# Delta-rule attention with a routed feed-forward layer: block 1's squares kept on chip, later blocks' squares and the zeroing moved in the written order

## The chip, the cores and the metric

One core of one Trainium2 chip runs the whole kernel. The metric is the device time of one launch in microseconds (us). The kernel before took 520.19 us (median of 3 runs, 515.07 to 524.5). A smaller number is better.

## The reference

For each of 4 batches and 8 heads (32 pairs, called lanes) a state of 48 x 48 is carried over 768 tokens. Keys are divided by their norm; at each token the output is read from the state, and then the state is corrected:

```
k_n = k / (norm(k) + 1e-6)
y[t]  = q[t] @ state
state = state + beta[t] * outer(k_n[t], v[t] - state.T @ k_n[t])
```

The heads' outputs, side by side, give 3072 tokens of width 384. A router (384 x 8) picks one of 8 experts for each token by the largest logit; the token's output is `gate * (relu(x @ w1[e]) @ w2[e])`, with w1 of 384 x 1024 and w2 of 1024 x 384, and the gate the softmax weight of the chosen expert.

## The kernel before

**Tiling.** The 768 tokens are 6 blocks of 128; a block is four sub-chunks of 32. A unit n = 4 * block + batch is one block of one batch, 24 in all; their tiles have that number (kt8 holds the keys of unit 8, gg8 its Gram). The main loop has 27 ticks t; a unit n passes through four ticks, sub-chunk q in tick n + q, so that four units are in work at a time. A tick has seven places, and place 7t + i is where `beside(t, i)` (L1121) writes extra work between the tick's own instructions.

**One tick.** `residual` (L490) multiplies keys with the states and with earlier corrections into the PSUM tile ks; VectorE (DVE) subtracts ks from the values v_all (L515). `chunk(ks_, t)` writes the Gram of a later unit (`kpart`, L249): 16 matmuls at L296, two ScalarE (ACT) copies at L278. `apply` (L517) multiplies the residual with wt, the inverted 32 x 32 triangular system of each lane (L523), and ACT copies the result out (L527). `finish` reads out y and updates the state; `qpart` makes the masked q-k products; `emit_x` forms the routed row. In ticks 0 to 3 the values of the next tick are scaled by ACT (L476, eight small instructions), later by DVE (L479).

**The inverses.** wt of a block is made on DVE, mostly by `Inverse` (L1009): `prepare` (norms out of the squared lengths, L342 to L369), `columns` (L395, L398) and `lanes` (products L421, reductions L427, a last transpose L432). Its steps are written a few at a time at the places, by a budget of 0.86 to 0.92 us each; what is left is written in one piece before `residual` of the tick that first needs wt (ticks 4, 8, 12, 16, 20). When the next block's inverse is ready too, the two alternate. `ROOT` names for each block three places: where `squares` is written (L318; its DVE instruction, L320, waits for the tile lg), where `root` is written (an ACT square root, L324), and from where the inverse may step. Block 0's inverse is made ahead of tick 0, with its last quarter by matmuls (`corner_products`, L438; L457, L464 on TensorE, L459, L468 on ACT).

**The squares' way.** lg holds, one lane beside the other, the 32 x 32 diagonal pieces of the Grams. For blocks 1 to 5 the last `kpart` of the block sends these pieces from gg to DRAM by four DMAs of 128-byte runs (gd, L284) and reads them back in the other layout by one DMA (lg, L288), which waits until the four have landed. All direct DMAs are issued by SyncE in written order: an instruction that waits holds back the loads of keys, queries, values and ku behind it. `KAT` gives the tick of a Gram's making where it is not n - 10.

**Zeroing.** The DRAM rows that routed tokens are gathered in (xg) are zeroed by seven DMAs of 788 KB each (L201): one behind gd of block 1, one behind gd of block 2, one each at the ends of ticks 2 and 4, one of tick 6 and two of tick 7.

**Before tick 0.** `fill` (L973) writes the Grams 4 to 7 of block 1 and 0 and 1 of block 0, each but the last with 13 or 12 idle matmuls (L777) behind it, beside block 0's columns on DVE. GpSimd (POOL) makes constants, masks (L307) and zeroes tiles, and `norms` lets it copy four 32 x 32 pieces into nt_all (L369), which the scaling of values needs. Behind the ticks the experts run, nearly bound by TensorE (PE) alone.

Of the kernel before, what the change touches and what calls it, by code (L numbers as in the profile page):

```python
# [8 lines left out]
F32 = mybir.dt.float32  # L9
# [9 lines left out]
B, H, S, D = 4, 8, 768, 48  # L19
C = 128  # L20
NT = S // C
NB = C // 32
# [19 lines left out]
def deltanet_moe(ctx, tc, kt_d, qt_d, kn_d, v_d, beta_d, w_gate, w1, w2, out):  # L42
    nc = tc.nc
# [67 lines left out]
    GB = 3  # L111
    KSL = 16
    LEAD = 10
    KAT = {8: 0, 9: 0, 2: 1, 10: 1, 3: 2, 11: 2, 12: 3, 13: 3}
    QSL = 4
    KTL = 17
    QTL = 6
# [2 lines left out]
    NB_ = 2  # L120
    LIVE = 7
    LAG = NB - 1
    FILL = 'k4 k5 k6 k7 k0', 'k1', '', ''

    ROOT = {1: (0, 1, 2), 2: (24, 27, 29), 3: (42, 45, 47), 4: (70, 73, 75), 5: (98, 101, 103)}
    FD = {"k4": 13, "k5": 13, "k6": 13, "k7": 13, "k0": 12}
    INIT = (0, 1, 2, 3, 'l', 'l', 'l')

# [3 lines left out]
    SPEND0 = (0.92,) * 7  # L132
    SPEND = (0.9,) * 7
    SPEND2 = (0.86,) * 7
    CL = (0, (0, 1), (0, 1))
    CLT = (2, 4)
    CLU = (6, 7, 7)
    W1 = 4
    DM2 = 0
    DEF = 2  # L140
# [18 lines left out]
    fp = ep_.enter_context(tc.tile_pool(name="fp", bufs=1, side="right"))  # L159
# [12 lines left out]
    gg_t = [gg_g[j // B][:, j % B] for j in range(KSL)]  # L172
# [13 lines left out]
    tiles = {tb: {b: {} for b in range(B)} for tb in range(NT)}  # L186
# [9 lines left out]
    def clear_slots(k):  # L196
        for x in [slots.pop(0) for _ in range(k)]:
            zero(x)
# [19 lines left out]
    def load_q(n):  # L218
        if n < NT * B:
            load_rows(qt_t[n % QTL], qt_d[n], n < QTL)  # L220
# [10 lines left out]
    def rows(t):  # L231

        if t < NB:
            return [slice(0, 32 * (t + 1))]
        return {NT * B: [slice(32, 64), slice(64, 128)], NT * B + 1: [slice(64, 128)],
                NT * B + 2: [slice(96, 128)]}.get(t, [slice(0, 128)])
# [13 lines left out]
    def kpart(n):  # L250

        tb, b = n // B, n % B
        kt, gg = kt_t[n % KTL], gg_t[n % KSL]
        V, A = nc.vector.tensor_copy, nc.scalar.copy
        if tb == 0:
            if n == 0:
                tiles["dg"] = fp.tile([128, BH, 32], F32, name="dg", tag="lg", bufs=3)
            dg = tiles["dg"]
            w = 64 if b < WIDE else 32
            db = [psg_[-1].tile([128, NP, w], F32, name=f"db{b}_0", tag="g"),  # L260
                  pss.tile([128, NP, w], F32, name=f"db{b}_1", tag="y", bufs=YB) if b < 2 else
                  pss.tile([128, NP, w], F32, name=f"db{b}_1", tag=f"sum{b - 2}")]
            for h in range(H):
                p, a = h // 2, h % 2
                r = slice(64 * a, 64 * a + 64)
                for i in range(0, C, w):
                    t = slice(i, i + w)
                    nc.tensor.matmul(db[a][t, p, :], lhsT=kt[r, p, t], rhs=kt[r, p, t], start=True, stop=True,
                                     tile_position=(64 * a, i), skip_group_check=True)
            for i in range(0, w, 32):  # L270
                for t in range(i, C, w) if w > 32 else (slice(0, C),):
                    t = t if w == 32 else slice(t, t + 32)
                    V(out=dg[t, b * H:(b + 1) * H:2], in_=db[0][t, :, i:i + 32])
                    A(out=dg[t, b * H + 1:(b + 1) * H:2], in_=db[1][t, :, i:i + 32])
            yield
        pg = halves(f"pg{tb}_{b}", kt, kt)
        for a in range(2):
            A(out=gg[:, a:H:2], in_=pg[a])  # L278
        if tb > 0 and b == B - 1:
            early_ = CL[tb] if tb < len(CL) else (0, 0)  # L280
            clear_slots(early_[0])
            for i in range(NB):
                r = slice(32 * i, 32 * i + 32)
                nc.sync.dma_start(out=gd[tb].rearrange("(i n) (r c) -> i r n c", i=NB, r=32)[i],  # L284
                                  in_=gg_g[tb % (KSL // B)].rearrange("p b h c -> p (b h) c")[r, :, r])
            tiles[tb]["lg"] = fp.tile([128, 32, 32], F32, name=f"lg{tb}", tag="lg", bufs=3)
            clear_slots(early_[1])
            nc.sync.dma_start(out=tiles[tb]["lg"].rearrange("p r c -> p (r c)"), in_=gd[tb])  # L288

    def halves(nm, kt, xt):  # L290

        pg = [psg_[-1].tile([128, NP, C], F32, name=f"{nm}_{a}", tag="g") for a in range(2)]
        for p in range(NP):
            for a in range(2):
                r = slice(64 * a, 64 * a + 64)
                nc.tensor.matmul(pg[a][:, p], lhsT=kt[r, p], rhs=xt[r, p], start=True, stop=True,  # L296
                                 tile_position=(64 * a, 0), skip_group_check=True)
        return pg

    def qpart(n):  # L300

        tb, b = n // B, n % B
        pm = pm_t[n % QSL]
        pg = halves(f"pq{tb}_{b}", kt_t[n % KTL], qt_t[n % QTL])
        for a in range(2):
            nc.scalar.copy(out=pm[:, a:H:2], in_=pg[a])  # L306
        nc.gpsimd.affine_select(out=pm, in_=pm, compare_op=ALU.is_gt, fill=0.0, base=0,  # L307
                                pattern=[[0, H], [1, C]], channel_multiplier=-1)
        yield

    def clear_w(tb):
        lw = tiles[tb]["lw"] = fp.tile([128, 32, 32], F32, name=f"lw{tb}", tag="lw", bufs=2)
        nc.gpsimd.memset(lw, 0.0)

    def squares(tb):

        T = tiles[tb]
        for k in ("ss", "s0", "r0"):  # L318
            T[k] = lp.tile([128, 32], F32, name=f"{k}{tb}", tag=k)
        nc.vector.tensor_scalar(out=T["ss"], in0=T["lg"].rearrange("p a b -> p (a b)")[:, 0:1024:33],  # L320
                                scalar1=1e-36, scalar2=None, op0=ALU.max)

    def root(tb):
        nc.scalar.activation(out=tiles[tb]["s0"], in_=tiles[tb]["ss"], func=AF.Sqrt, scale=0.25)  # L324
# [146 lines left out]
    def scale_v(t, act=False):  # L471

        vn = vt[t]
        for r in rows(t):
            for h in range(H if act else 0):
                nc.scalar.activation(out=vn[r, h], in_=vn[r, h], func=AF.Copy, scale=nt_t[r, t * H + h:t * H + h + 1])  # L476
            if act:
                continue
            nc.vector.tensor_tensor(out=vn[r], in0=vn[r], in1=nt_t[r, t * H:(t + 1) * H].unsqueeze(2)  # L479
                                    .broadcast_to([r.stop - r.start, H, D]), op=ALU.mult)  # L480
# [277 lines left out]
    def run(gen, steps=1):  # L758

        for _ in range(steps):  # L760
            if next(gen, tiles) is tiles:
                return False
        return True
# [8 lines left out]
    def dummy(k, w=512):  # L772

        if k:
            wm = pss.tile([128, w], F32, name=f"wm{next(cnt)}", tag="y", bufs=YB)
        for _ in range(k):
            nc.tensor.matmul(wm, lhsT=busy[:, 0:128], rhs=busy[:, 0:w], start=True, stop=True)  # L777
# [163 lines left out]
    clear_w(0)  # L941

    ks_ = [(KAT.get(n, n - LEAD), kpart(n), n) for n in range(NN)]
    qs_ = [(n - QSL + NB, qpart(n)) for n in range(NN)]
    dummy(5)
# [20 lines left out]
    for n in range(NB_):  # L966
        load_ku(n)
    clear_slots(CL[0])
    while "nt" not in tiles[0]:
# [6 lines left out]
    def fill(xs):  # L976
        for x in xs.split():
            n, part = int(x[1:]), (ks0 if x[0] == "k" else qs0)
            if part[n] and not run(part[n]):
                done.add(x)  # L980
            dummy(FD.get(x, 0), 16)

    fill(FILL[0])
    for n in range(LEAD, LEAD + 2):
        load_k(n)
    router()
    fill(FILL[1])
    lane = columns(0)
    run(lane, 12)
    for _ in norms(0):  # L990
        pass
    scale_v(0, act=True)
    run(lane, 100)
    turns = corner_products(0)
    run(turns)
    fill(FILL[2])
    run(turns)
    fill(FILL[3])
    ks_ = sorted((x for i, x in enumerate(ks_) if f"k{i}" not in done), key=lambda x: (x[0], x[2]))
    qs_ = [x for i, x in enumerate(qs_) if f"q{i}" not in done]  # L1000
    class Inverse:
# [13 lines left out]
        def ready(self, t):  # L1015
            if self.at == -12:
                return place[0] >= ROOT[self.tb][2]
            return not ("cols" in tiles[self.tb] and t < B * self.tb - 1)
# [43 lines left out]
    def beside(t, i):  # L1062

        place[0] = 7 * t + i
        for tb in ROOT:
            if place[0] == ROOT[tb][0]:
                squares(tb)
            if place[0] == ROOT[tb][1]:
                root(tb)
# [10 lines left out]
    for t in range(NN + LAG):  # L1080
# [43 lines left out]
        if t >= LAG:  # L1124
            load_q(t - LAG + QTL)
        clear_slots(CLT.count(t))
        clear_upper(CLU.count(t))
    i = 0
# [181 lines left out]
    if True:  # L1310
        ind, sel, t8 = small("ind"), small("sel"), small("t8")
        ei, j0, ce, r, rc, gi, ov = (small(n_, (128, 1)) for n_ in ("ei", "j0", "ce", "r", "rc", "gi", "ov"))
# [63 lines left out]
        for f in range(KF):  # L1376
# [4 lines left out]
                                     in_=yo, in_offset=None, bounds_check=N - 1, oob_is_err=False)  # L1381
# [40 lines left out]
```

## Time and profile before

| | before |
|---|---|
| median of 3 runs | 520.19 us |
| the profiled execution | 521.66 us |
| its span, first to last instruction | 519.9 us |
| mean granted TensorE clock | 0.946 |
| PE busy | 469.9 us, 90% |
| DVE busy | 311.9 us, 60% |
| ACT busy | 270.8 us, 52% |
| POOL busy | 157.0 us, 30% |

The profiled execution lies 1.47 us above the median; 1.76 us of it are outside the span. In the timelines and tables below times are in us from the span's start. A granted clock of 1.00 is 2.4 GHz, and of 0.5 is 1.2 GHz; a value between means that a stretch had both. PE is busy nearly everywhere, so what one looks for are the stretches in which it is not, or in which its clock is low.

### The profile page before, as it was taken

How to read it: one execution, taken by the hardware profiler on the slowest of the kernel's cores; microseconds unless marked ns; L12 is line 12 of the kernel's file. 1: busy time of each engine (PE TensorE's matmuls, PEld its weight loads, DVE VectorE, ACT ScalarE, POOL GpSimd, SP SyncE). 2: the span in 40 equal slices, each digit the busy share in tenths (PEclk: the TensorE clock that was granted, in tenths of full speed). 3: DMA queues.
4: the chain of work that ended last, by engine and by line, in shares of the span. 5: the costliest groups of instructions: out<-in, count | busy, mean ns of one | idle time of the engine just before them, and what ended most of it. 6: DMA issues, size and time to landing. Idle time of an engine off the chain costs nothing. (4 is left out here: it accounts for less than half of the span.)

```text
span 519.9 us, 18283 instructions
## 1 busy us (share of the span) xinstructions
PE 469.9 (90%) x7724; PEld 432.9 (83%) x7724; DVE 311.9 (60%) x717; ACT 270.8 (52%) x600; POOL 157.0 (30%) x342
## 2 busy tenths in 40 slices
PE   6898869788789669997889999999999999999995
PEld 4788758677677558786679899999999999999995
DVE  5839495798487498954554386646382746436330
ACT  4567845565547436576644255645363636344330
POOL 6111124477446556873030211020201111110202
PEclk9869979999879978998999989999999999999999
DMA  8780765974724713363431156655364746354001
GB/s 244 183 239 4 198 178 127 272 201 108 198 76 102 168 65 109 95 222 122 119 100 57 38 171 203 183 172 177 115 212 127 224 129 198 126 178 127 35 3 43
DMA packets 57151, 73.39 MB, mean 141 GB/s; under 512 B 25929, under 2 KB 44831, under 8 KB 57056
## 3 DMA queue, kind: packets, MB, share of 16 engines
q1 hardware_dynamic: 53600, 62.44, 42.4%
q0 software_dynamic: 3456, 9.57, 5.1%
q8 instruction: 75, 1.23, 1.0%
q14 instruction: 20, 0.16, 0.1%
HBM read 54.15 MB, written 18.62 MB: 140 GB/s over the span
## 5 line engine op out<-in xcount | busy, mean ns | idle before, releaser
L861 PE MATMUL y<-w2h,hx 128*128 128x384 f32 x352 | 93.5, 340 | 0.1
L864 POOL DMA_INDIRECT out_dram<-yo,idx x32 | 30.7, 959 | 198.8 <-ACT yo L1201 96.0
L784 DVE TENSOR_TENSOR w2l<-w2r,w2h 128x768 fp32r<-128x768 f32 x32 | 31.3, 980 | 72.9 <-ACT w2h L783 72.7
L861 PEld LDWEIGHTS y<-w2h,hx 128*128 128x128 f32 x352 | 64.1, 188 | 0.4 <-issue 0.4
L527 ACT COPY u<-ks 32x384 f32<-32x384 f32 x96 | 45.1, 470 | 34.3 <-PE ks L523 32.7
L861 PE MATMUL y<-w2l,hx 128*128 128x384 f32 x176 | 59.3, 337 | 0.0
L850 PE MATMUL h<-xl,w1h 128*128 128x416 f32 (+2 forms) x168 | 57.3, 341 | 0.2 <-DVE xl L784 0.2
L850 PE MATMUL h<-xh,w1h 128*128 128x416 f32 (+2 forms) x168 | 57.3, 341 | 0.0
L850 PE MATMUL h<-xh,w1l 128*128 128x416 f32 (+2 forms) x168 | 57.2, 341 | 0.0
L853 ACT ACTIVATE hx<-h 128x448 fp32r<-128x448 f32 (+1 forms) x64 | 32.8, 517 | 33.3 <-PE h L850 32.4
L1201 ACT ACTIVATE yo<-y,gt 128x384 f32<-128x384 f32 x22 | 12.8, 582 | 69.1 <-PE y L861 57.8
L523 PE MATMUL ks<-v_all,wt 32*32 32x48 f32 x1536 | 28.7, 222 | 22.0 <-DVE v_all L515 21.5
L307 POOL TENSOR_SCALAR_AFFINE_SELECT pm<-pm 128x1024 f32<-128x1024 f32 x24 | 27.1, 1131 | 67.7 <-ACT pm L306 67.5
L496 PE MATMUL ks<-st,kt 128*32 128x96 f32 x768 | 43.7, 250 | 3.2 <-issue 1.7
L523 PEld LDWEIGHTS ks<-v_all,wt 32*32 32x32 f32 x1536 | 24.5, 119 | 25.9 <-DVE v_all L515 23.4
L854 DVE SCALAR_TENSOR_TENSOR hx<-h,hx 128x448 fp32r<-128x448 f32 (+1 forms) x64 | 36.8, 586 | 14.6 <-ACT hx L853 14.4
L296 PE MATMUL pg<-kt 64*128 64x128 f32 x384 | 35.6, 318 | 2.6 <-ACT gg L278 1.6
L496 PEld LDWEIGHTS ks<-st,kt 128*32 128x32 f32 x768 | 32.4, 110 | 6.5 <-ACT u L527 1.9
L278 ACT COPY gg<-pg 128x512 f32<-128x512 f32 x48 | 25.8, 588 | 20.9 <-PE pg L296 20.1
L599 POOL DMA_INDIRECT xg<-row,sli x24 | 28.4, 1182 | 25.9 <-ACT yt L570 8.0
L784 DVE TENSOR_TENSOR w1l<-w1r,w1h 128x1024 fp32r<-128x1024 f32 x24 | 29.4, 1224 | 9.8 <-ACT w1h L783 6.5
L296 PEld LDWEIGHTS pg<-kt 64*128 64x128 f32 x384 | 30.2, 218 | 5.5 <-ACT gg L278 2.5
(205 smaller groups left out, 1050.3 us busy)
## 6 DMA issues: line engine op xcount, KB each, us to landing
w1r<-in_w_dram SPq DMA_DIRECT2D x24, 512.0 KB, 3.6
w2r<-in_w_dram SPq DMA_DIRECT2D x32, 384.0 KB, 3.5
xg<-zrow SPq DMA_DIRECT2D x7, 788.0 KB, 6.8
kt<-in_kt_dram SPq DMA_DIRECT2D x17, 256.0 KB, 5.8
xr<-xg SPq DMA_DIRECT2D x7, 591.0 KB, 5.0
ku<-in_kn_dram SPq DMA_DIRECT2D x20, 192.0 KB
qt<-in_qt_dram SPq DMA_DIRECT2D x36, 96.0 KB, 2.6
v_all<-in_v_dram SPq DMA_DIRECT2D x15, 192.0 KB
```

The costliest lines, as they stand in the source:

```text
L296: nc.tensor.matmul(pg[a][:, p], lhsT=kt[r, p], rhs=xt[r, p], start=True, stop=True, tile_position=(64 * a, 0), skip_group_check=True)
L307: nc.gpsimd.affine_select(out=pm, in_=pm, compare_op=ALU.is_gt, fill=0.0, base=0, pattern=[[0, H], [1, C]], channel_multiplier=-1)
L496: nc.tensor.matmul(ks[32 * q:32 * q + 32, 2 * p:2 * p + 2, :], lhsT=kt_t[n % KTL][:, p, 32 * q:32 * q + 32], rhs=st_view(n % B, p), start= ...
L523: nc.tensor.matmul(ks[r, h, :], lhsT=tiles[n // B]["wt"][r, n % B * H + h, :], rhs=vn[r, h, :], start=True, stop=True, tile_position=(32 * ...
L527: nc.scalar.copy(out=uview(n)[r], in_=ks[r])
L599: put = nc.gpsimd.indirect_dma_start(out=xg, out_offset=bass.IndirectOffsetOnAxis(ap=at, axis=0), in_=x, in_offset=None, bounds_check=OFF ...
L784: nc.vector.tensor_tensor(out=lo, in0=src, in1=hi.bitcast(F32), op=ALU.subtract)
L850: nc.tensor.matmul(ps, lhsT=w[:, d, fs], rhs=x_[:, d], start=(n == 0), stop=(n == len(terms) - 1))
L853: nc.scalar.activation(out=hh, in_=ps, func=AF.Relu)
L854: nc.vector.scalar_tensor_tensor(out=hl, in0=ps, scalar=0.0, in1=hh.bitcast(F32), op0=ALU.max, op1=ALU.subtract)
L861: nc.tensor.matmul(ps, lhsT=h(f)[h_], rhs=w2[w][:, f, :], start=(n == 0), stop=(n == len(terms) - 1))
L864: nc.gpsimd.indirect_dma_start(out=out, out_offset=bass.IndirectOffsetOnAxis(ap=idx, axis=0), in_=yo, in_offset=None, bounds_check=N - 1, ...
```

## The change

Block 1's squares no longer go through DRAM. Behind each Gram of block 1 GpSimd copies the four 32 x 32 diagonal pieces of its eight heads together (16 copies of 32 x 256 in all) into the tile of Gram 12, which is not yet in use, and DVE transposes it into lg (`compact`), behind the first part of `corner_products`. Its squares and root are written there too, and its inverse may step from place 0.

The Gram 7 is written behind block 0's norms, and Grams 0 and 1 behind the scaling of tick 0's values; the idle matmuls become 48 columns wide instead of 16. Grams 10 and 11 are made in tick 1, 2 and 12 in tick 2, 3 and 13 in tick 3. The squares, root and first step of blocks 3, 4 and 5 are written some five places later. The seven zeroings go to the ends of ticks 0 (two), 1, 2 (two) and 3 (two).

```diff
-    KAT = {8: 0, 9: 0, 2: 1, 10: 1, 3: 2, 11: 2, 12: 3, 13: 3}
+    KAT = {8: 0, 9: 0, 10: 1, 11: 1, 2: 2, 12: 2, 3: 3, 13: 3}
...
-    FILL = 'k4 k5 k6 k7 k0', 'k1', '', ''
-
-    ROOT = {1: (0, 1, 2), 2: (24, 27, 29), 3: (42, 45, 47), 4: (70, 73, 75), 5: (98, 101, 103)}
+    FILL = 'k4 k5 k6', 'k7', 'k0 k1'
+
+    ROOT = {1: (-1, -1, -1), 2: (24, 27, 29), 3: (47, 49, 51), 4: (75, 77, 79), 5: (103, 105, 107)}
...
-    CL = (0, (0, 1), (0, 1))
-    CLT = (2, 4)
-    CLU = (6, 7, 7)
+    CL = (0, (0, 0), (0, 0))
+    CLT = (0, 0, 1, 2)
+    CLU = (2, 3, 3)
...
-        if tb > 0 and b == B - 1:
+        if tb == 1:
+            sq = gg_t[KSL - B]
+            for i in range(NB):
+                r = slice(32 * i, 32 * i + 32)
+                nc.gpsimd.tensor_copy(sq.rearrange("p h (g c) -> p (h g) c", c=32)[r, b * H:(b + 1) * H], gg[r, :, r])
+        if tb > 1 and b == B - 1:
...
+    def compact(tb):
+
+        lg = tiles[tb]["lg"] = fp.tile([128, 32, 32], F32, name=f"lg{tb}", tag="lg", bufs=3)
+        nc.vector.transpose(out=lg, in_=gg_t[KSL - B].rearrange("p h (g c) -> p c (h g)", c=32))
...
-            dummy(FD.get(x, 0), 16)
+            dummy(FD.get(x, 0), 48)
...
-    fill(FILL[1])
     lane = columns(0)
     run(lane, 12)
     for _ in norms(0):
         pass
+    fill(FILL[1])
     scale_v(0, act=True)
+    fill(FILL[2])
     run(lane, 100)
     turns = corner_products(0)
     run(turns)
-    fill(FILL[2])
+    compact(1)
+    squares(1)
     run(turns)
-    fill(FILL[3])
+    root(1)
```

## Rows read from the trace of the kernel before

**Rows 1.** Page, part 1: busy time, share of the span, instructions of an engine.

```profile
PE 469.9 (90%) x7724; PEld 432.9 (83%) x7724; DVE 311.9 (60%) x717; ACT 270.8 (52%) x600; POOL 157.0 (30%) x342
```

**Rows 2.** Table of stretches (start:end): length, busy times, granted clock, DMA.

```profile
core 0: us, PE busy (x) PEld busy (x) DVE busy (x) ACT busy (x) POOL busy (x), PEclk, DMA share, GB/s
25.90:62.65 36.75, 33.42 (x968) 29.63 (x961) 22.94 (x53) 27.65 (x81) 5.65 (x12) 0.86 0.51 142
62.65:78.70 16.05, 10.84 (x234) 9.36 (x233) 12.41 (x29) 7.79 (x22) 3.33 (x7) 0.79 0.73 192
78.70:86.90 8.20, 7.86 (x236) 6.88 (x234) 5.75 (x22) 5.72 (x14) 3.55 (x11) 1.00 0.55 144
...
95.10:107.60 12.50, 9.64 (x234) 8.32 (x232) 12.47 (x23) 6.29 (x16) 6.20 (x9) 0.86 0.77 224
...
126.70:134.90 8.20, 7.96 (x238) 6.97 (x237) 1.67 (x2) 5.29 (x13) 5.88 (x20) 1.00 0.65 128
134.90:150.70 15.80, 11.65 (x234) 10.02 (x232) 13.54 (x22) 6.75 (x17) 4.97 (x13) 0.68 0.54 153
...
167.95:174.86 6.91, 6.91 (x225) 6.09 (x224) 1.29 (x2) 4.18 (x11) 4.51 (x14) 1.00 0.60 135
174.86:189.45 14.59, 8.23 (x218) 7.12 (x216) 12.25 (x23) 5.59 (x15) 5.28 (x11) 0.77 0.53 129
189.45:199.80 10.35, 8.23 (x223) 7.16 (x221) 9.80 (x27) 4.79 (x12) 6.95 (x21) 0.84 0.21 63
...
62.65:107.60 44.95, 36.30 (x934) 31.54 (x932) 32.56 (x78) 25.53 (x65) 17.99 (x41) 0.89 0.69 185
```

**Rows 3.** Waits: PE's from 20 to 250, then DVE's; us, times, longest.

```profile
PE ks L523 <- DVE v_all L515: 20.2, 7, 4.5
...
DVE ss L320 <- DMA lg<-gd: 28.3, 5, 7.5
```

**Rows 4.** Timeline of DVE: the squares of blocks 1 to 5; start, duration, instruction.

```profile
30.95 0.19 DVE L320 TENSOR_SCALAR ss<-lg 128x32 f32<-128x32 f32 x1 [3.57 <-DMA lg<-gd]
...
64.78 0.19 DVE L320 TENSOR_SCALAR ss<-lg 128x32 f32<-128x32 f32 x1 [5.19 <-DMA lg<-gd]
...
94.39 0.19 DVE L320 TENSOR_SCALAR ss<-lg 128x32 f32<-128x32 f32 x1 [5.14 <-DMA lg<-gd]
...
136.62 0.19 DVE L320 TENSOR_SCALAR ss<-lg 128x32 f32<-128x32 f32 x1 [7.55 <-DMA lg<-gd]
...
177.17 0.19 DVE L320 TENSOR_SCALAR ss<-lg 128x32 f32<-128x32 f32 x1 [6.88 <-DMA lg<-gd]
```

**Rows 5.** Timeline of PE: the first product with block 1's inverse, in tick 4.

```profile
71.93 1.51 PE L523 MATMUL ks<-v_all,wt 32*32 32x48 f32 x64 [4.49 <-DVE v_all L515]
```

**Rows 6.** Timeline of SyncE's queue: block 2's squares out and back.

```profile
51.10 3.27 SPq L284 DMA_DIRECT2D gd<-gg  x4
...
59.06 0.34 SPq L288 DMA_DIRECT2D lg<-gd  x1
```

**Rows 7.** Timeline ahead of tick 0: ACT on Gram 7, its scaling, a DVE transpose.

```profile
18.91 1.07 ACT L278 COPY gg<-pg 128x512 f32<-128x512 f32 x2 [0.57 <-PE pg L296]
...
23.18 1.91 ACT L476 ACTIVATE v_all<-v_all,nt_all 32x48 f32<-32x48 f32 x8
...
8.51 1.94 DVE L334 STREAM_TRANSPOSE lg<-dg 128x1024 f32<-128x1024 f32 x1
```

**Rows 8.** Timeline: GpSimd's work and DVE's two-input instructions beside it.

```profile
17.20 1.19 POOL L369 COPY nt_all<-r 32x32 f32<-32x32 f32 x4 [6.78 <-DVE r L365]
...
17.37 0.29 DVE L395 TENSOR_TENSOR tmp<-lg,lw 128x128 f32<-128x128 f32 x1
...
38.27 1.09 POOL L307 TENSOR_SCALAR_AFFINE_SELECT pm<-pm 128x1024 f32<-128x1024 f32 x1
...
38.44 1.04 DVE L395 TENSOR_TENSOR tmp<-lg,lw 128x96 f32<-128x96 f32 x1
39.51 0.26 DVE L398 TENSOR_TENSOR lw<-lw,tmp 128x96 f32<-128x96 f32 x1
```

## The prediction

> **What bounds the kernel now.** The page's busy shares come first [rows 1]: PE is at 90%, DVE at 60%, so as a mean the kernel is PE's. The table by ticks shows where that fails [rows 2]. An undisturbed tick takes 8.20 us at clock 1.00, or 6.91 when no Gram is left to make; tick 4 takes 16.05, tick 7 12.50, tick 11 15.80, tick 15 14.59 and tick 16 10.35, at clocks of 0.68 to 0.86. So what is lost there is lost twice: PE waits, and the clock is then part of the time at the lower level of 1.2 GHz. The wait lists name the link [rows 3]: PE waited 20.2 us for DVE's subtraction, and DVE 28.3 us, five times, for lg, the squares coming back from DRAM. The timeline has these five [rows 4]. DVE works in written order, so while L320 waits for lg, the rest of the running inverse and the next subtraction stand behind it. Four ticks of DVE work are 32.56 us (the last stretch of [rows 2]), against 4 x 8.20 = 32.8 of undisturbed PE: DVE has nothing to spare, and what it waits, PE pays at the block's end. Tick 4 shows it: block 2's squares hold DVE until 64.78, block 1's inverse comes late, and PE starts the product with it at 71.93 after 4.49 idle [rows 4, 5].
>
> **Before tick 0.** GpSimd gets 16 copies of 32 x 256, 12 of them ahead of the norms' copies. The trace has none of that size. Bounds: 0.30 us each (four of 32 x 32 in 1.19) and 1.09 (a select of 1024 columns) [rows 8]; I take 0.5, nearer the small one, as 256 columns are a quarter of 1024. Gram 6 was copied out by ACT at 18.34 (0.57 ahead of Gram 7's copies [rows 7]); its four pieces end at 20.3 and the norms' copies at 21.5, where they ended at 18.4. The scaling now stands in ACT's queue behind Gram 7 (19.98) and ahead of Grams 0 and 1. It runs 21.5 to 23.4, the two Grams' copies to about 26 (2 x 1.07, and PE's Gram 1 waits for a buffer of Gram 0), where ACT had been through with all of it at 25.1. So tick 0 starts 1.1 us late; with copies of 0.30 it is 0.3, with 1.09 it is 3.4. Gram 7's pieces end at 23.5, ahead of DVE's transpose (1.94 [rows 7]), which fills time in which DVE stood idle; the squares were late till 30.95 [rows 4], and that wait of 3.57 goes. The wider idle matmuls lie in PE's gaps; I cost them at nothing, bounds -1 to +1, for what the clock does. In SyncE's queue the four gd DMAs of block 1, a zeroing and the lg read that waited for them go; the loads behind them come sooner, and the two zeroings of tick 0 stand behind every load that ticks 0 and 1 need.
>
> **Ticks 0 to 3** have DVE busy 22.94 of 36.75 us, ACT 27.65 [rows 2]: a chain through ACT, whose work is the same. They keep their length. Block 1's inverse starts some 4 us earlier at least and has two places more.
>
> **Tick 4.** Grams 10 and 11 in tick 1 send block 2's squares out one tick earlier, about 8.5 us. Before, from the first DMA to landing took 64.78 - 51.10 = 13.7 us, with a zeroing between gd and lg [rows 6, 4]; none stands there now. So lg is there at 56 to 57, and DVE comes to the squares at 59.6 (64.78 - 5.19). The 5.19 us wait goes, and the remaining inverse fits in front of tick 4's subtraction. Tick 4 takes 8.45 instead of 16.05: 7.6 us won. Grams 2 and 3 only change places with them (16 matmuls, two ACT copies each), so a tick's load stays. SyncE now waits in tick 1 for Gram 11 and then for gd to land, and the loads of keys 13 and 14 and three zeroings stand behind: I expect key 13 at about 57, when tick 3 needs it (bounds: 0, or 1 us late; I take 0).
>
> **The later steps.** Blocks 3, 4 and 5 kept DVE waiting from 2.4 us into ticks 6, 10 and 14, until 7.5, 9.9 and 9.2 us into them [rows 4, 2]. Five places of 0.9 (0.86 in block 5) bring 4.5 us (4.3) of real inverse work in front, so DVE arrives at 6.9 (6.7): waits of 0.6, 3.0 and 2.5 are left of 5.14, 7.55 and 6.88. What is behind the wait is now close: two places, then the next subtraction. In tick 6 landing plus two places (1.8) is 9.3, before the subtraction's turn at 10: free. Tick 7 falls from 12.50 to 8.3: 4.2 won. In tick 10 it is 11.7, with the subtraction 12.3; PE needs it at 12.1. Tick 11 loses 0.2; as block 4's inverse starts four places later, more of block 3's stands in one piece at tick 12, 9.7 us of DVE work against 8.2, which costs 1.4. Ticks 10 and 11, 24.0 before, become 18.0: 6.0 won. In ticks 14 to 16 the undisturbed tick is 6.91, DVE's 10.4 of work in tick 15 does not fit, and I get 3 x 6.91 + 1.8 (squares) + 3.1 (work) + 1.4 (lower clock) = 27.0 instead of 31.85: 4.85 won. Block 5's later start costs about 0.5 at tick 20.
>
> **Sum:** 7.6 + 4.2 + 6.0 + 4.85 - 1.1 - 0.5 = 21.05 us, from 521.66: 500.6, said as 501. The experts behind are PE's own and move as a whole. That execution lies 1.5 us above the median shown; the three runs span 9.4, so I leave it there and add 4 us at the range's ends.
>
> **A rule against the change.** Beside GpSimd's select at 38.27 a DVE instruction with two SBUF inputs took 1.04 us, its neighbour of the same size 0.26; but beside the four small copies at 17.20 such a one took 0.29, no longer than elsewhere [rows 8]. I count no contention. The Trainium skill (GPSIMD Engine Reference, section 1, Specifications) says that GpSimd shares its SBUF interfaces with VectorE and that instructions with two SBUF inputs contend; block 0's columns, beside which the copies run, are of this kind. The first of the two rows agrees with it, the second does not. This is the third rival below.
>
> **Rivals.**
> First, DVE stays full: the squares still land late and, now right in front of a subtraction, hold it. For: lg needed 9.9 and 9.2 us in ticks 10 and 14, and there is no slack in the 32.56. Against: in tick 6 it landed at 7.5. Then blocks 4 and 5 win nothing: 521.66 - 7.6 - 4.2 + 1.1 = 511. Chance 0.16.
> Second, with the zeroing gone from ticks 4 to 7 and block 1's small packets gone, lg lands in ticks 10 and 14 as in tick 6, at 7.5: the left waits go, each followed by its share of lower clock: some 4 us more, 497. Chance 0.12.
> Third, the copies hold block 0's columns: 12 x 0.5 = 6 us on DVE, of which about 2 hide behind ACT's longer way, so tick 0 is 4 us later still: 505. Chance 0.12.
> Fourth, it doesn't do what it says for block 2: three zeroings, at the ends of ticks 1 and 2, run beside lg and the loads of keys 13 and 14, and tick 3 or 4 waits for them as long as before: 521.66 - 13.5 = 508. Against: SyncE issues the lg read ahead of them. Chance 0.06.
> Fifth, slower: GpSimd's strided copies are far dearer. They stand ahead of the norms, on which ACT's scaling and behind it Grams 0 and 1, the corners and tick 0 wait. POOL had 6.78 us idle there [rows 8], so 12 copies of c us push tick 0 back by 12c - 6.8. All that is won, 22 us, is gone at c = 2.4; at c = 3 it is 29.2, or 529. Against: the longest row beside it is 1.09 for four times the columns. Chance 0.04.
>
> **Numbers.** The forecast, 501, has 0.50, with 495 to 507 of its own. The range 493 to 512 runs from the second rival less 4 us to just past the first; it leaves out the fifth and the runs' far ends. About what a measurement can tell from no change is 2%, 10.4 us, so faster means under 509.8: nearly all of the forecast, second and third, somewhat under half of the first and over half of the fourth: 0.82. Slower than 530.6 is the fifth with yet dearer copies or a bad start: 0.04. Within 2%: 0.14.
>
> **What would show it.** In the changed trace: GpSimd copies of about 0.5 us at the new line and DVE's columns beside them no longer than 0.29; tick 0 at 26 to 28; L320 of block 1 at about 27 with no wait, that of block 2 with none, those of blocks 4 and 5 with 2 to 3 us; ticks 4 and 7 near 8.3 at clock 1.00, tick 15 still long. The prediction is wrong if PE still idles over 2 us for L515 in tick 4, if tick 0 starts after 30, or if ticks 11 and 15 keep their 15.80 and 14.59.

## The result and the profile after

The changed kernel takes 514.61 us (median; 508.67 to 517.6) where the kernel before took 519.85 (515.07 to 525.79) on the same chip: a ratio of 0.988, 95% interval 0.985 to 0.991. Medians and ranges are over all executions, but ratios compare only those in the faster of two states that executions fall into, so here and below a ratio is not the quotient of the two medians. It is faster by 1.2%, less than the 2% that I had called measurable, and outside the predicted range. The profiled execution took 512.92 us (span 510.7), against the 521.66 that the sum was made from: 8.7 us won instead of 21.05. (It lies 1.7 below its median, the one of before 1.8 above; that is the difference between 8.7 and 5.2.)

The page's busy line of the changed kernel, as [rows 1]:

```profile
PE 469.9 (92%) x7724; PEld 432.5 (85%) x7724; DVE 315.8 (62%) x718; ACT 270.7 (53%) x600; POOL 171.6 (34%) x358
```

POOL has 16 instructions and 14.6 us more; the compacting copies are 6.5 of it, the rest is spread over GpSimd's other instructions and was not followed up. PE is busy for the same time to the tenth, so the 9.2 us that the span lost are PE's idle time. The table of stretches shows where (columns as in [rows 2]); a stretch is a tick, and the first row is ticks 0 to 3 together, then ticks 4, 7, 8, 11, 15, 16 and 19:

```profile
27.40:66.10 38.70, 35.15 (x973) 31.02 (x961) 27.97 (x61) 27.61 (x81) 7.11 (x12) 0.82 0.38 98
...
66.10:79.90 13.80, 9.96 (x236) 8.47 (x234) 6.88 (x22) 7.92 (x23) 3.25 (x7) 0.88 1.05 302
...
96.50:105.90 9.40, 8.36 (x234) 7.27 (x232) 7.75 (x14) 5.90 (x16) 6.97 (x12) 1.00 0.86 211
105.90:117.20 11.30, 9.60 (x238) 8.39 (x236) 10.82 (x29) 6.02 (x15) 6.99 (x22) 0.85 0.33 99
134.50:144.10 9.60, 8.32 (x237) 7.09 (x237) 8.33 (x15) 6.04 (x16) 5.84 (x13) 1.00 0.77 200
167.90:175.70 7.80, 7.07 (x218) 6.03 (x216) 7.54 (x14) 4.84 (x14) 6.91 (x10) 1.00 0.96 245
175.70:189.20 13.50, 9.84 (x225) 8.43 (x226) 11.81 (x30) 5.06 (x13) 7.57 (x24) 0.75 0.25 71
203.80:214.00 10.20, 8.72 (x221) 7.39 (x219) 9.91 (x13) 4.87 (x13) 7.12 (x17) 0.83 0.35 112
```

Against [rows 2] tick 11 fell from 15.80 to 9.60, tick 15 from 14.59 to 7.80 and tick 7 from 12.50 to 9.40: the later steps work. Tick 4 only fell from 16.05 to 13.80. Ticks 0 to 3 grew from 36.75 to 38.70, and ticks 8, 16 and 19 are longer than they were (9.3, 10.35 and 8.2). The wait lists of the changed kernel, PE's first, as [rows 3] (20 to 250 us; total, times, longest):

```profile
PE ks L533 <- DVE v_all L525: 8.9, 5, 3.1
PE ks L506 <- issue: 2.9, 3, 2.3
PE yp L556 <- issue: 2.6, 2, 1.6
...
DVE ss L330 <- DMA lg<-gd: 1.5, 3, 0.8
```

DVE's wait for the squares is down from 28.3 to 1.5, PE's for DVE from 20.2 to 8.9. What has grown is "issue", PE standing still for nothing that the profile can name. The kernel before had these two at the same products:

```profile
PE ks L496 <- issue: 1.7, 2, 1.3
...
PE yp L546 <- issue: 0.3, 1, 0.3
```

The five squares on DVE's timeline, as [rows 4]:

```profile
29.22 0.19 DVE L330 TENSOR_SCALAR ss<-lg 128x32 f32<-128x32 f32 x1
...
62.47 0.17 DVE L330 TENSOR_SCALAR ss<-lg 128x32 f32<-128x32 f32 x1
...
96.43 0.19 DVE L330 TENSOR_SCALAR ss<-lg 128x32 f32<-128x32 f32 x1 [0.39 <-DMA lg<-gd]
...
134.02 0.19 DVE L330 TENSOR_SCALAR ss<-lg 128x32 f32<-128x32 f32 x1 [0.81 <-DMA lg<-gd]
...
168.34 0.19 DVE L330 TENSOR_SCALAR ss<-lg 128x32 f32<-128x32 f32 x1 [0.26 <-DMA lg<-gd]
```

Block 2's squares, at 62.47, wait for nothing: the wait of 5.19 is gone as forecast. In place of PE's wait of 4.49 for DVE [rows 5], tick 4 has these two on PE's timeline, and no wait for DVE:

```profile
69.59 0.27 PE L506 MATMUL ks<-st,kt 128*32 128x96 f32 x1 [2.26 <-issue]
...
75.28 0.54 PE L556 MATMUL yp<-qt,st 64*64 64x128 f32 x9 [1.57 <-issue]
```

About then, from 58 to 73 us, SyncE's queue issues five zeroings of 788 KB, where the kernel before has two from 54 to 63 (at a DMA share of 0.73 in tick 4 [rows 2]); they stand here with their start and issue time:

```profile
58.19 0.43 SPq L201 DMA_DIRECT2D xg<-zrow  x1
...
62.32 0.99 SPq L201 DMA_DIRECT2D xg<-zrow  x2
...
70.22 3.20 SPq L201 DMA_DIRECT2D xg<-zrow  x2
```

The DMA share of tick 4 is 1.05 (table above; it can pass 1, as a packet counts whole where it starts): the engines are full from its first to its last slice. The first account, then, is that zeroing, by filling the DMA engines, stops PE's own issue. The DMA part of the page counts a queue of its own, "q8 instruction", 75 packets in the span on the same 16 engines, and a program that arrives late would look like this. Rivals: the squares or PE's other inputs are late in a way the list doesn't name; or the later steps alone make the gain, and tick 4 is noise.

### The profile page after: what moved, and what is told of

Its sections match the earlier page's. It is cut to its first block, busy times and chain, and to the rows that moved or that the text cites. A ratio compares the mean times of both kernels' runs of the same rounds, so it can differ in the third digit from the quotient of the medians.

```text
span 510.7 us, 18291 instructions
## 1 busy us (share of the span) xinstructions
PE 469.9 (92%) x7724; PEld 432.5 (85%) x7724; DVE 315.8 (62%) x718; ACT 270.7 (53%) x600; POOL 171.6 (34%) x358
## 3 DMA queue, kind: packets, MB, share of 16 engines
q8 instruction: 75, 1.23, 1.1%
## 5 line engine op out<-in xcount | busy, mean ns | idle before, releaser
L537 ACT COPY u<-ks 32x384 f32<-32x384 f32 x96 | 45.1, 470 | 20.3 <-PE ks L533 14.4
L312 POOL TENSOR_SCALAR_AFFINE_SELECT pm<-pm 128x1024 f32<-128x1024 f32 x24 | 27.9, 1164 | 66.0 <-ACT pm L311 65.8
L506 PE MATMUL ks<-st,kt 128*32 128x96 f32 x768 | 45.0, 252 | 4.4 <-issue 2.9
L864 DVE SCALAR_TENSOR_TENSOR hx<-h,hx 128x448 fp32r<-128x448 f32 (+1 forms) x64 | 36.9, 587 | 14.5 <-ACT hx L863 14.4
L533 PE MATMUL ks<-v_all,wt 32*32 32x48 f32 x1536 | 27.1, 207 | 11.2 <-DVE v_all L525 9.3
L609 POOL DMA_INDIRECT xg<-row,sli x24 | 27.2, 1134 | 25.3 <-ACT yt L580 8.0
L525 DVE TENSOR_TENSOR v_all<-v_all,ks 128x384 f32<-128x384 f32 (+3 forms) x28 | 15.4, 551 | 32.8 <-PE ks L518 28.3
L533 PEld LDWEIGHTS ks<-v_all,wt 32*32 32x32 f32 x1536 | 22.4, 108 | 15.6 <-DVE v_all L525 10.6
```

The lines of the kernel that those rows point to most:

```text
L506: nc.tensor.matmul(ks[32 * q:32 * q + 32, 2 * p:2 * p + 2, :], lhsT=kt_t[n % KTL][:, p, 32 * q:32 * q + 32], rhs=st_view(n % B, p), start= ...
L533: nc.tensor.matmul(ks[r, h, :], lhsT=tiles[n // B]["wt"][r, n % B * H + h, :], rhs=vn[r, h, :], start=True, stop=True, tile_position=(32 * ...
L537: nc.scalar.copy(out=uview(n)[r], in_=ks[r])
L609: put = nc.gpsimd.indirect_dma_start(out=xg, out_offset=bass.IndirectOffsetOnAxis(ap=at, axis=0), in_=x, in_offset=None, bounds_check=OFF ...
L864: nc.vector.scalar_tensor_tensor(out=hl, in0=ps, scalar=0.0, in1=hh.bitcast(F32), op0=ALU.max, op1=ALU.subtract)
```

## The experiments

Each time stands beside the kernel before on the same chip: 519.27 us for the first four, 516.63 for the next four, 519.45 for the last three.

**1. All zeroings behind the end of tick 0** (changed kernel):

```
-    CLT = (0, 0, 1, 2)
-    CLU = (2, 3, 3)
+    CLT = (0, 0, 0, 0)
+    CLU = (0, 0, 0)
```

> The changed kernel with all seven zeroings at the end of tick 0. Theory A (full queues): in the changed kernel the four zeroings of ticks 2 and 3 keep the DMA engines at a share of 1.0 from 60 to 80 us, PE's program comes through the same engines, and PE stops in tick 4 for 2.26 and 1.57 us with the releaser 'issue'. Then here tick 4 takes 8.5 to 10 us with no such gap above 0.6, gaps of that kind may turn up in ticks 0 to 2, and the total is 509 to 512. Theory B (own program): these gaps belong to PE's way through its program and were hidden behind DVE's wait before; then tick 4 stays at 13 to 14 us and the total at 513 to 516.

Measured: 510.05 us, ratio 0.984 [0.976, 0.992]. Tick 4 lasts 8.3 with no gap; tick 3, with gaps of 0.80 and 1.19, lasts 11.1. No zeroing is issued after 31 us here; the loads of keys, queries and values alone have the DMA engines at a share of 0.88 from 54 to 64.3 us. So it need not be zeroing.

**2. The zeroings late** (changed kernel):

```
-    CLT = (0, 0, 1, 2)
-    CLU = (2, 3, 3)
+    CLT = (0, 0, 2, 4)
+    CLU = (6, 7, 7)
```

> The changed kernel with the zeroings two at the end of tick 0, one each of ticks 2 and 4, one of tick 6, two of tick 7. Theory A: ticks 2 to 4 have two zeroings instead of five, so tick 4 takes 9 to 11 us, and a gap of about 1.3 us comes back in tick 8 or 9, as in the kernel before; total 510 to 513. Theory B: tick 4 stays at 13 to 14 us, total 513 to 516.

Measured: 509.25 us, ratio 0.984 [0.974, 0.994]. Tick 4 lasts 9.3 with one gap of 0.88, at a DMA share of 0.36. The time lies under the 510 to 513 expected, and the gap expected back in tick 8 or 9 is not there. Both moves, earlier and later, cure the tick but for the 0.88, and in both block 2's squares run when they did in the changed kernel (62.62 and 61.65, there 62.47). So it is the traffic in it, not its order. The whole is 2 to 5 us better than the changed kernel (by the ratios the one, by the medians the other); ticks 8 and 16, at 11.5 and 11.7, are still long.

**3. The steps of blocks 3 to 5 put back** (changed kernel):

```
-    ROOT = {..., 3: (47, 49, 51), 4: (75, 77, 79), 5: (103, 105, 107)}
+    ROOT = {..., 3: (42, 45, 47), 4: (70, 73, 75), 5: (98, 101, 103)}
```

> The changed kernel with the squares, roots and first steps of blocks 3 to 5 where they were before. If the later steps are what won (theory C), DVE waits 5 to 7 us again for lg of blocks 3, 4 and 5, ticks 7, 11 and 15 are at 12 to 16 us again, and the total is 523 to 528, slower than the kernel before. If the steps only moved the waits (theory D), the total stays at 514 to 517.

Measured: 520.82 us, ratio 1.004 [0.999, 1.009]. The two waits in it (same columns as above):

```profile
PE ks L533 <- DVE v_all L525: 15.9, 6, 4.1
...
DVE ss L330 <- DMA lg<-gd: 15.2, 3, 5.7
```

Three waits of 5.71, 5.00 and 4.53 are back, and ticks 7, 11 and 15 last 14.5, 13.9 and 13.7. The time is under the 523 to 528 expected, and not clearly slower than the kernel before: all of the change but this line is worth nothing, within half a per cent.

**4. Only the later steps, in the kernel before:**

```
-    ROOT = {..., 3: (42, 45, 47), 4: (70, 73, 75), 5: (98, 101, 103)}
+    ROOT = {..., 3: (47, 49, 51), 4: (75, 77, 79), 5: (103, 105, 107)}
```

> The kernel before with the later squares, roots and first steps of blocks 3 to 5 and nothing else of the change. Theory C: ticks 4 and before as in the kernel before, tick 4 at 16 us; ticks 7, 11 and 15 at 8 to 10 us; total 507 to 511, faster than the whole change, because all its other parts together lose 1.4 us up to tick 7 by the trace. Theory D: 517 to 521.

Measured: 508.77 us, ratio 0.980 [0.972, 0.989]. This one line has as good a ratio as any kernel here. Ticks 7, 11 and 15 last 9.2, 10.3 and 11.7 (8 to 10 expected), tick 4 still 15.1. DVE's wait for squares, 9.2 in all, is left mostly in the blocks that the line doesn't touch (3.67 and 3.24 for blocks 1 and 2):

```profile
PE ks L523 <- DVE v_all L515: 13.3, 9, 3.5
PE ks L496 <- issue: 4.2, 4, 2.7
...
DVE ss L320 <- DMA lg<-gd: 9.2, 5, 3.7
```

**5. Block 1 by way of DRAM as before; Grams 10 and 11 and the later steps kept** (kernel before; the new lines):

```
+    KAT = {8: 0, 9: 0, 10: 1, 11: 1, 2: 2, 12: 2, 3: 3, 13: 3}
+    ROOT = {1: (0, 1, 2), 2: (24, 27, 29), 3: (47, 49, 51), 4: (75, 77, 79), 5: (103, 105, 107)}
+    CL = (0, (0, 1), (0, 0))
+    CLT = (0, 0, 0)
```

> The kernel before with block 1's squares through DRAM as they were, its fill and its idle matmuls, but with Grams 10 and 11 in tick 1, the later steps of blocks 3 to 5, and zeroings one behind gd of block 1, three at the end of tick 0, one of tick 6, two of tick 7. Theory E (the on-chip way of block 1 wins nothing; the earlier lg of block 2 and the later steps win all): tick 0 starts at 25 to 26, ticks 0 to 3 as before, tick 4 at 8.5 to 10 us, ticks 7, 11, 15 at 9 to 12; total 500 to 505. Theory F (block 1's early start is needed for tick 4): tick 4 keeps over 12 us, with PE waiting for DVE, total 506 to 511.

Measured: 505.06 us, ratio 0.982 [0.974, 0.990]. Tick 4 lasts 8.3 without a compacting copy. Block 1's wait of 3.57 [rows 4] was thus not what held it. The early ticks missed what was expected: tick 0 starts at 27.9, not 25 to 26, and ticks 0 to 3 last 41.5, not 36.75. Ticks 1 and 2 take 10.8 and 10.2, with a gap of 0.85 at 47.28; the three zeroings behind tick 0 are the likely cause, and number 9, where they are spread, has 9.0 and 8.7.

**6. More inverse work in each place** (number 5):

```
-    SPEND = (0.9,) * 7
-    SPEND2 = (0.86,) * 7
+    SPEND = (1.0,) * 7
+    SPEND2 = (1.0,) * 7
```

> The one before this, with a budget of 1.0 instead of 0.9 and 0.86 us of inverse steps a place from tick 4 on, so that less is written in one piece ahead of ticks 8, 12, 16 and 20. If that piece is what is left of PE's waits for DVE (about 1.7 us in tick 8 and 3.1 in tick 15 or 16, with the lower clock behind them), these waits fall under 1 us and the total is 3 to 5 us below it. If DVE's work as a whole is the bound, the waits only spread over the ticks and the total is within 1.5 us of it.

Measured: 510.14 us, ratio 0.991 [0.986, 0.996]: no gain, and neither of the two outcomes expected, as number 5 beside it has 505.06 and 0.982. The two intervals overlap, so a loss isn't shown either; where the time goes is left open.

**7. The idle matmuls at their old width** (number 2): `dummy(FD.get(x, 0), 48)` becomes 16.

> The changed kernel with the zeroings in ticks 0, 0, 2, 4, 6, 7, 7 (as e2_zero_late) and the idle matmuls 16 columns wide again. If the wider ones cost or win something ahead of tick 0, the start of tick 0 moves by 0.5 to 1.5 us from its 27.3, and the length of the stretch at clock 0.50 that follows from its 16 us; if they lie in gaps, both stay within 0.4 and 1 us, and the total at 508 to 511.

Measured: 507.12 us, ratio 0.985 [0.972, 0.999]; tick 0 at 26.9 where number 2 has 27.3, and the stretch at clock 0.50 that follows is 17.1 us long in both. Inconclusive on the whole; the width costs nothing that I can see, as taken.

**8. Each compacting copy made twice** (number 2):

```
+                for _ in range(2):
-                nc.gpsimd.tensor_copy(sq...[r, b * H:(b + 1) * H], gg[r, :, r])
+                    nc.gpsimd.tensor_copy(sq...[r, b * H:(b + 1) * H], gg[r, :, r])
```

> As e2_zero_late, with each of GpSimd's 16 copies made twice (the same values again). If the copies set the start by GpSimd's order (norms behind Gram 6's copies, ACT's scaling behind the norms) and by holding DVE's columns beside them, the columns take 12 us or more (10.3 in the changed kernel, 8.6 before) and tick 0 starts at 30 to 31.5 instead of 27.3; if they lie beside other work, it starts at 27 to 28.

Measured: 508.14 us, ratio 0.988 [0.982, 0.995]. The timeline of GpSimd in it:

```profile
16.42 7.14 POOL L284 COPY gg<-gg 32x256 f32<-32x256 f32 x16 [1.40 <-ACT gg L278]
23.61 0.97 POOL L380 COPY nt_all<-r 32x32 f32<-32x32 f32 x4
```

Sixteen take 7.14, 0.45 each. The norms' copies start at 23.61, tick 0 at 30.4, 3.1 later than with single copies: so doubled, the copies stand on the path to tick 0, as the fifth rival put it, at a fifth of its price. It is GpSimd's order that does it, not DVE: the columns take 11.3, not the 12 or more expected, and PE waits 3.88 for ACT's Gram copies, which stand behind the norms and the scaling. (Tick 3 has a gap of 1.93 here too and lasts 14.4.)

What stood open by then was whether traffic by itself makes the gaps, and what a kernel without either loss takes. **9. The zeroings one by one** (number 5): `CLT = (0, 0, 0)` becomes `(0, 2, 4)`.

> The kernel before with the later steps of the inverses, Grams 10 and 11 in tick 1, block 1 still by way of DRAM, and zeroings spread thin: one in tick 0 with block 1's squares, one at the end of tick 0, one at the ends of ticks 2 and 4, the last three in ticks 6 and 7. Theory A (what is still lost in ticks 1 to 4 is lost to DMA traffic in front of PE's own instruction loads, and the on-chip way for block 1 costs more in the startup than it saves): tick 0 starts at 25 to 27, tick 4 lasts 8.2 to 9.3, ticks 1 and 2 about 9 each where the kernel with three zeroings in tick 0 had 10.8 and 10.2; in all 500 to 505. Rival B (zeroing's place in ticks 0 to 3 is worth nothing beyond noise and the gain of 10 us is all that the later steps give): 507 to 510.

Measured: 506.62 us, ratio 0.981 [0.968, 0.993]. A half miss. Tick 4 lasts 8.2 and tick 1 9.0, but tick 0 starts at 27.8, not 25 to 27, and tick 3 lasts 12.9 with gaps of 1.09, just ahead of the zeroing issued at 58.89, and 1.27, behind it. The first, as in number 1, thus comes with loads alone.

**10. Three zeroings made again on rows already zero, at the ends of ticks 2 and 3** (number 2):

```
+        for n in range((0, 0, 1, 2)[t] if t < 4 else 0):
+            zero(part(0, 4, n * C, n * C + C))
```

> The kernel with the zeroing late (changed kernel, of which tick 4 lasted 9.3), with three zeroings made again, rows that are zero already: one at the end of tick 2 and two at the end of tick 3, so that what DMA carries there is about as in the changed kernel; 2.4 MB more to write and nothing else. Theory A (traffic itself stops PE's issue in tick 4): PE waits for its own instructions 2 us or more in all between 64 and 80 us, tick 4 lasts 12 to 14.5, the time is 512 to 516. Rival B (the late zeroing won for another reason, a load or a square that came sooner): tick 4 stays at 8.3 to 9.5, the time within 2 us of 509.

Measured: 512.79 us, ratio 0.995 [0.987, 1.003]. Tick 4 on PE's timeline:

```profile
69.27 0.27 PE L506 MATMUL ks<-st,kt 128*32 128x96 f32 x1 [0.61 <-issue]
...
76.57 0.48 PE L556 MATMUL yp<-qt,st 64*64 64x128 f32 x9 [3.20 <-issue]
```

Nothing but writes of zeros was added, and the gaps are 3.81 us in all, where number 2 had 0.88; tick 4 is 12.1 where it was 9.3. Two of the lines that the DMA view of that tick (67.5 to 79.5, in 40 slices of 0.3 us, busy tenths) gives:

```profile
DMA  9899788999999999999999951000000002000658
...
q8 instruction: 2, 0.03, 1.0%
```

The engines run full until 74.4 and are idle from 75; PE stands from 73.37 to 76.57 and goes on behind that.

**11. As 9, none at the end of tick 2 and two at the end of tick 4:** `CLT = (0, 4, 4)`.

> As the spread kernel, but with no zeroing at the end of tick 2 and two at the end of tick 4. Theory A: ticks 3 and 4 have no gap of PE's issue over 0.5 us and last 17.5 or less together; two zeroings behind tick 4 may bring one gap of 1 to 2 us into ticks 5 or 6 (the two together 16.5 to 19); in all 500 to 506. Rival B (gaps in PE's issue have nothing to do with the zeroing): ticks 3 to 6 as in the spread kernel within 0.5 us each.

Measured: 504.59 us, ratio 0.982 [0.965, 0.999], the lowest median of all. Its stretches (ticks 0 to 3, tick 4, tick 9):

```profile
26.10:63.70 37.60, 33.40 (x969) 29.69 (x960) 26.39 (x58) 27.64 (x81) 5.28 (x11) 0.86 0.59 160
63.70:72.00 8.30, 7.94 (x234) 6.92 (x232) 7.15 (x20) 7.49 (x22) 3.26 (x7) 1.00 0.34 108
106.40:120.20 13.80, 10.93 (x235) 9.39 (x233) 8.05 (x27) 5.80 (x15) 7.39 (x20) 0.75 0.45 111
```

Tick 0 starts at 26.1, ticks 1 and 2 last 8.7 each, ticks 3 and 4 have no gap in PE's issue. Together these two last 18.2, not the 17.5 expected: tick 3 waits 1.10 for keys. The two zeroings behind tick 4 cost ticks 5 and 6 nothing (8.3 and 8.2), which the traffic account allowed but did not ask for. Tick 9 pays instead:

```profile
109.76 0.38 PE L496 MATMUL ks<-st,kt 128*32 128x96 f32 x3 [2.57 <-issue]
```

That gap stands behind the zeroings issued at 92.06 and 98.55 (two). In number 4 (2.66 at 115.09) and number 5 (1.87 at 114.7) it follows three zeroings likewise. In the changed kernel, which has none there, tick 9 has only 0.43. But numbers 2, 7 and 10 have three zeroings too, and no gap of 0.5 in tick 9: that they come first is not enough.

## Why the prediction was wrong

**The step that failed is tick 4**: "Tick 4 takes 8.45 instead of 16.05: 7.6 us won" came out as 2.3. Its reasoning on DVE held: squares without a wait, the inverse early (block 1's last piece at 65.53), no wait of PE for DVE. And 8.45 is what the tick takes (8.2 to 9.3) in numbers 1, 2, 5, 7, 9 and 11. What it missed is what is late next: I counted three zeroings, at the ends of ticks 1 and 2, and weighed them against lg and the keys alone, at 0.06 in the fourth rival. There are five by the end of tick 3, and their victim is PE's issue: 3.83 us of gaps, and behind them a stretch at a lower clock, 0.88 over the tick, so the two levels of 2.4 and 1.2 GHz were both granted. Numbers 1 and 2 take the traffic out, and the gaps go or shrink to 0.88; number 10 puts it back and they return. I count that as shown. None of the three signs that were to show the prediction wrong came (PE idle for L515 in tick 4, tick 0 after 30, ticks 11 and 15 as long as before): the loss lay where none of them looked.

**What the gap is,** the times of the DMA packets in the traces show. The queue "q8 instruction" brings 75 packets of 16 KB, 1.23 MB for the page's 18291 instructions; by that estimate one holds some 245 instructions. The two gaps of tick 4 stand 252 PE instructions apart, and the second cuts a run of 16 products at L556 on one unit's tiles after the seventh, so no operand was late. In the changed kernel such packets land at 68.09 and 73.98, and PE goes on at 69.59 and 75.28; in number 10 they land at 67.78 and 75.22, and PE goes on at 69.27 and 76.57. The 13 profiles have 60 gaps of 0.5 us or more put down to "issue" in the first 260 us, and each ends 1.2 to 1.7 us behind such a landing. So PE waited for its program. In the traffic the packets of tick 4 started 4.4 and 3.2 us after PE had passed the place some 252 instructions earlier, in number 11 only 0.9 and 1.5. In the kernel before one started 3.8 us after that place and landed at 68.53, but PE stood for DVE until 71.93 and needed it at 73.65: the wait for DVE covered it. That the packets queue behind the data is inferred from these times and from number 10; the trace doesn't show when they were asked for.

**Startup and ticks 0 to 3** were to lose 1.1 and lost 3.5 by tick 4 (tick 0 at 27.4 instead of 25.9; 38.70 instead of 36.75). The copies cost 0.43 to 0.46 each, under the 0.5 taken. What failed is "I count no contention". GpSimd and DVE in the changed kernel, side by side on the timelines:

```profile
17.60 1.71 POOL L283 COPY gg<-gg 32x256 f32<-32x256 f32 x4 [0.73 <-ACT gg L278]
19.37 1.13 POOL L379 COPY nt_all<-r 32x32 f32<-32x32 f32 x4
20.56 1.82 POOL L283 COPY gg<-gg 32x256 f32<-32x256 f32 x4
```

```profile
19.06 0.39 DVE L408 TENSOR_TENSOR lw<-lw,tmp 128x126 f32<-128x126 f32 x1
19.48 0.29 DVE L405 TENSOR_TENSOR tmp<-lg,lw 128x128 f32<-128x128 f32 x1
...
21.18 0.42 DVE L408 TENSOR_TENSOR lw<-lw,tmp 128x120 f32<-128x120 f32 x1
...
22.54 0.26 DVE L405 TENSOR_TENSOR tmp<-lg,lw 128x96 f32<-128x96 f32 x1
```

Beside the large copies DVE's columns mostly take 0.39 to 0.42, beside the small ones 0.29, and 0.26 when the copies are over. The columns end at 24.6 instead of 22.0, and PE stands still for them:

```profile
25.73 0.73 PE L467 MATMUL co<-wt,dg 32*32 32x16 f32 x64 [1.77 <-DVE wt L457]
```

The small copies of [rows 8] had been the wrong witness; the select of 1.09 beside the 1.04 was the right one. The rule that I had set beside them (the Trainium skill, GPSIMD Engine Reference, section 1, Specifications: interfaces shared with VectorE) agrees with the rows beside the large copies, though not with those beside the small: it was the better guide. The third rival was thus real in kind, but small: PE waits 1.77 here, 0.73 before, and tick 0 comes 0.4 later than the 27.0 forecast, not 4. In numbers 1, 2 and 7, which have the same copies, PE waits 1.3 to 1.4 for ACT's Gram copies there instead, with tick 0 at 26.9 to 27.3. Most of the miss is that ticks 0 to 3 did not keep their length: tick 1 takes 9.8 instead of 8.7, as the lower clock at which tick 0 runs lasts longer into it (0.82 over the tick; before, 0.99 from 37 to 47 us); and tick 3 has a gap of 0.65.

**Ticks 5 to 7** were to win 4.2 and won 2.9 (tick 7 9.4, not 8.3). **Ticks 8 and 9**, which I left out, lost 1.3: what is moved out of tick 7 is DVE work in tick 8, 10.82 busy of 11.30. I had seen that only for the later blocks. (Number 4, with the same later steps, has 8.7 in tick 8, so the steps alone don't do it.) **Ticks 10 to 12** gave 6.3 against 6.0 (26.0 long, 26.2 forecast): right, though by other shares, since lg came sooner than I thought (0.81 of wait instead of 3.0), as the second rival has it. **Ticks 14 to 16** are 28.1 long, not 27.0. Tick 15 is free and tick 16 pays, at 11.81 of DVE work. **From tick 17 to 20** 2.1 was lost, not 0.5: tick 19 with 9.91 of DVE's 10.20. The misses add up: 5.3 in tick 4, 2.4 before it, 1.3 in ticks 5 to 7, 1.3 in 8 and 9, about 1 in 14 to 16 and 1.6 at the end are 12.9. Less 0.3 won back in ticks 10 to 12 and 0.8 in tick 22, and with 0.5 lost outside the span, that is the 12.3 between 21.05 and 8.7.

**The first rival** ("DVE stays full", 511) gave nearly the time, for another reason: the squares were not late. But its premise, no slack in DVE, fits ticks 8, 16 and 19, where DVE is busy for most of the time (10.82 of 11.30, 11.81 of 13.50, 9.91 of 10.20); number 6, which only spread DVE's work otherwise, won nothing. That is argued, not shown.

**Where the gain went,** then: the later steps are worth about 10 us by themselves (number 4), and number 3 shows that the rest adds nothing. Its win in tick 4 is paid for by its zeroings, in the startup and ticks 0 to 3, and by DVE in ticks 8, 16 and 19, which last 11.3, 13.5 and 10.2 (in number 4 8.7, 7.3 and 8.4, though tick 15 has 11.7 there and 7.8 here). Moving the zeroings out of ticks 2 and 3 gives back 2 to 5 us (the ratios, 0.984 against 0.988, have intervals that overlap; number 10 beside number 2, 0.995 against 0.984, has the same sign). Number 11, with neither the copies nor those zeroings, is by its ratio some 9 us below the kernel before. By its interval it can't be told from numbers 4, 5 and 9; all four have 0.980 to 0.982.

**Not settled:** the gap in PE's issue near 13 us, ahead of tick 0, is between 1.60 (changed kernel) and 5.22 (number 5) in these profiles, 2.54 before, and may move tick 0 by a microsecond or two, though number 9 has 2.04 and starts at 27.8, as late as number 5. It too ends behind the landing of an instruction packet, the first: at 11.17, 13.08 and 11.54 in these three, with PE going on at 12.65, 14.49 and 12.98. What sets that landing is open.

## What to carry to other kernels

Before a bulk transfer is moved to where "nothing waits for it", add up what the DMA engines then carry in each stretch: at a share near 1.0 an engine that needs none of the data can stop, as its program comes over the same engines, and the profile calls that only "issue". Instruction packets that land just ahead of the gap's end tell it. A wait removed in front of a full engine wins no more than its next idle place allows, so ask at each block's end how much of that engine's work is left for the tick behind. And test the parts of a bundled change alone: here one line of it was the whole gain, within what the intervals can tell.

## What the runs showed of the hardware

- PE stops without a named cause in heavy DMA traffic, in the ticks 0.5 to 3.2 us at a time. Tick 4 lasted 13.8 at a DMA share of 1.05, 12.1 at 0.66 (full in its first half), 9.3 at 0.36 and 8.3 at 0.34. The share alone does not decide it: before, 0.73 brought no such gap (PE stood still for DVE there, which covered one), and two zeroings issued at 72.05 (number 11) brought none in the two ticks behind them, the first at a share of 0.94.
- Such a gap ends 1.2 to 1.7 us behind the landing of a 16 KB packet of the queue "q8 instruction", in 60 of 60 gaps of 0.5 us or more. It falls at the same few places of PE's program in every profile, neighbouring ones 250 to 256 PE instructions apart, as the two of tick 4 at 252.
- A GpSimd copy of 32 x 256 took 0.43 us, and a two-input DVE instruction beside it about 0.1 us more, as in 0.42 instead of 0.28 for 128 x 120; copies of 32 x 32 left DVE's time alone.
